# Gating one token quarter early instead of two, and starting the block products one head group later, in a fused attention and gated-MLP kernel

## The chip, the cores and the metric

The kernel runs on one core of one Trainium2 chip. The metric is the device time of one execution in microseconds; less is better. The engines are TensorE (PE, with its weight loads shown apart as PEld), VectorE (DVE), ScalarE (ACT), GpSimd (POOL) and SyncE (SP), whose queue issues nearly all DMAs.

## The reference

2048 tokens of width 512; 32 heads of width 128 over a cache of 2048 keys; all tensors in bf16.

```python
xn = layernorm(x)
# s: attention with cached keys and values
q = (xn @ wq) per head;  p = softmax(q @ k.T * 128 ** -0.5);  s = concat_heads(p @ v) @ wo
# g: silu of a two-stage MLP on the same xn
h  = gelu(layernorm(xn) @ w1), its four column blocks shifted by +1, -1, +2, -2 tokens
x1 = xn + h @ w2
g  = silu(x1 + gelu(layernorm(x1) @ w3) @ w4)
return x + s * g
```

## The kernel before

**Tiling.** Tokens lie in 16 tiles t of 128, and in four quarters qt of 512 (four tiles each). Heads lie in eight groups g of four (HG = 4, NG = 8, QT = 4). One *unit* is one head hh of one group on one quarter: u = 16 g + 4 qt + hh, 128 units, 0 to 127, in that order. A unit has eight *slots* p (SPU = 8), each with two of the 16 key tiles; slot n is 8 u + p.

**Head of the kernel.** The first normalisation, the MLP and its gate g (kept in `xall`, one tile per t, as twice the gate) come first, for quarters 0 and 1 in full; the last matmuls of quarters 2 and 3 (`held_mm`) are spread over the first eight units. When these are done a pool `pS` opens, in which the attention sums live. The queries of units 0 to 10 and 127 are made ahead (`made`).

**A slot of the main loop** (`for n in range(UB * SPU)`, line 904). Two score matmuls into one of two score tiles (`s_slot`), an exp on ScalarE over 1024 columns (L416), and two value matmuls of ten slots earlier (`pv_run`). The rest of a unit's work is placed by slot:

- On VectorE the softmax sums: `add_first` (L422), three `add_next` (L427), `fold` (L431) and `fold_last` (L435), a transpose by DMA, `turned_sums` (L465, L467), a broadcast of the reciprocals by DMA, and `norm` (L485), which scales the value product and frees its bank. For the last four units the sums are taken by four small matmuls on TensorE instead (`sums`, tile ps_sum).
- The queries of a later unit. *Plain:* four matmuls of 512 columns (`q_mm`) and one copy on VectorE (`q_copy`, L327). *Block products:* for a pair of units v, v+1 (two heads), seven products (`product`, k = 1 to 7) of two matmuls with 256 columns each in place of eight, and four steps on VectorE that combine them (`q_part`, six operations, L388 to L400). They need sums of blocks of xn (`x_sum`, L352, four per quarter) and differences of blocks of the weights (`w_sum`, L361, four per pair of heads). Product k = 4 stands one slot after `q_part` 2 (L397, L398), in the odd unit, and writes the bank that this step reads.
- The output projection: once the four heads of a (g, qt) are normalised, one token tile of it is made per unit (`wo_slot`): four matmuls and `wo_post`, which adds the result to `sacc[t]` on VectorE (L537 for the first group, L549 for the others).

Plain queries are placed in slots 3 to 6 two units ahead, up to the pair FIRST. From unit FIRST - 2 to LAST the wo matmuls have places that go round the products; elsewhere they have the default places, slots 3 to 6, and their result is taken in slot 7 or 0.

**The gate in `wo_post`.** With `LATE` and `GY` a quarter can be gated before its last head group. For a tile of a LATE quarter, at group GY - 1 the sum is scaled by the gate (`y_scale`, L515) and the residual added (`y_add`, L520), after its load (`fin_load`), all at later slots, one step of one tile per unit. In the groups from GY on, the wo result is gated on its own (L542) and then added: to the sum (L545) or, in the last group, in `y_out` (L524) when `pay` runs it. For any other tile, the last group does all at once: add (L549), gate (L558), residual (L560), and the output's DMA. Its residual is loaded behind the tile before it (`wo_slot`), the first one when the quarter's last head is normalised (`norm_queue`).

**The end** (from line 971) is an order written out by hand: unit 127 in halves, the last tiles of quarter 2's output projection, and then quarter 3's, whose four tiles have code of their own (`last_stt` to `last_whole`) and always use the early gate.

Every engine runs its instructions in the order in which the program issues them, and so does SP with its DMAs, so an operation that waits holds what was issued behind it.

Of the kernel before, what the change touches and what calls it, by code (L numbers as in the profile page):

```python
# [17 lines left out]
def kernel(  # L18
# [21 lines left out]
    _, H, Sk, Dh = A_k_cache.shape  # L40
# [4 lines left out]
    QT = Sq // 512  # L45
# [5 lines left out]
    HG = 4  # L51
    NG = H // HG

    SPU = KC // 2
# [68 lines left out]
    HEAD = 7  # L123
    XS = 3 * QT + 1
    units = [(g, qt, hh) for g in range(NG) for qt in range(QT) for hh in range(HG)]
    LATE = (QT - 2, QT - 1)
    GY = NG - 2
    NU = len(units)
    TURN = range(NU - HG)
    NS = NU * SPU  # L130
# [3 lines left out]
    def at(n, fn):  # L134
        todo[n].append(fn)
# [201 lines left out]
    def x_block(qt, half, dcs):  # L337
        c = qt * 512 + 256 * half
        return xnT[:, dcs, c:c + 256]

    def x_sum(qt, i):
        if i == 2 and qt < QT - 1:
            out = x_block(qt, 1, LO)
        else:
            out = pS.tile([P, 2, 256], BF16, tag="xs", bufs=XS, name="xs")[:]
        a, b, op = (
            (x_block(qt, 1, LO), x_block(qt, 1, HI), ALU.add),
            (xs.get((qt, 0)), x_block(qt, 0, LO), ALU.subtract),
            (x_block(qt, 0, LO), x_block(qt, 1, LO), ALU.subtract),
            (x_block(qt, 0, HI), xs.get((qt, 1)), ALU.subtract),  # L350
        )[i]
        pin(nc.vector.tensor_tensor(out=out, in0=a, in1=b, op=op))  # L352
        xs[qt, i] = out

    def w_sum(h, i):
        if i == 0:
            wc[h] = pS.tile([P, 4, 2, Dh], BF16, tag="wc", bufs=2, name="wc")
        w, o = wc[h], [wc[h][:, k] for k in range(4)]
        b11, b12, b21, b22 = (wqs[h + j][:, d, :] for d in (LO, HI) for j in (0, 1))
        a, b = ((b12, b11), (b22, o[0]), (b22, b12), (b21, o[1]))[i]  # L360
        pin(nc.vector.tensor_tensor(out=o[i], in0=a, in1=b, op=ALU.subtract))  # L361
# [147 lines left out]
    def fin_load(t):  # L509
        xl = token(False, "xl")  # L510
        pin(nc.sync.dma_start(out=xl[:], in_=xsrc[t]))
        fin[t] = xl
# [20 lines left out]
    def wo_post(g, t, n):  # L533
        ps = wo_box.pop(0)
        if g == 0:
            sacc[t] = pS.tile([P, D], FP32, tag="sacc", bufs=NT, name="sacc")
            pin(nc.vector.tensor_copy(out=sacc[t][:], in_=ps[:]))  # L537
            return
        sa, gl = sacc[t][:], xall[:, t, :]
        if t // 4 in LATE and g >= GY:  # L540
            tm = pS.tile([P, D], FP32, tag="tm", bufs=2, name="tm")
            pin(nc.vector.scalar_tensor_tensor(  # L542
                out=tm[:], in0=ps[:], scalar=0.5, in1=gl, op0=ALU.mult, op1=ALU.mult))
            if g < NG - 1:
                pin(nc.vector.tensor_tensor(out=sa, in0=sa, in1=tm[:], op=ALU.add))  # L545
            else:
                owed.append((t, tm))
            return
        pin(nc.vector.tensor_tensor(out=sa, in0=ps[:], in1=sa, op=ALU.add))  # L549
        if t // 4 in LATE and g == GY - 1:  # L550
            k = n + SPU * (t - 4 * LATE[0]) + 1
            at(max(k - SPU, n + 1), lambda: fin_load(t))
            at(k, lambda: y_scale(t))
            at(k + SPU, lambda: y_add(t))
        if g < NG - 1:
            return
        xl = fin.pop(t)
        pin(nc.vector.scalar_tensor_tensor(  # L558
            out=gl, in0=sa, scalar=0.5, in1=gl, op0=ALU.mult, op1=ALU.mult))
        pin(nc.vector.tensor_tensor(out=xl[:], in0=gl, in1=xl[:], op=ALU.add))  # L560
        pin(nc.sync.dma_start(out=out2d[t * P:(t + 1) * P, :], in_=xl[:]))
# [253 lines left out]
    for g in range(NG - 1):  # L815
        b = (g * QT + QT - 1) * HG
        for hh in range(HG):
            h = (g + 1) * HG + hh
# [35 lines left out]
    def norm_queue(u):  # L854
        norm(u)
        gg, qq, hh = units[u]
        if hh == HG - 1:
            wo_todo.extend((gg, 4 * qq + ts) for ts in range(4))
            if gg == NG - 1 and qq not in LATE:
                fin_load(4 * qq)  # L860
# [3 lines left out]
    def wo_slot(part, n, each=2, **kw):  # L864
# [5 lines left out]
        wo_post(gg, t, n)  # L870
        if gg == NG - 1 and t % 4 < 3 and t + 1 not in fin and t // 4 not in LATE:
            fin_load(t + 1)

    FIRST, LAST = 12, NU - 4
    pairs = range(FIRST, LAST + 1, 2)
    q_plan = defaultdict(list)
    steps = defaultdict(list)
# [9 lines left out]
            if fn is which:  # L887
                fn(v, k)

    for qt, u in ((QT - 1, 8), (0, 10), (1, 14), (2, 18)):  # L890
        for i in range(4):
            at((u + i // 2) * SPU + 1 + 4 * (i % 2), lambda qt=qt, i=i: x_sum(qt, i))
    for h in range(0, H, 2):
        u = (h // HG) * QT * HG + (-4, -2)[h % HG // 2]
        for i in range(4):
            n = max(u, 8) * SPU if h < HG else (u + i // 2) * SPU
            at(n + (2, 6)[i % 2] + (i // 2) * (h < HG) + 8 * (h % HG == 2) * (h < HG), lambda h=h, i=i: w_sum(h, i))

    for v in range(1, NU):
        if v not in made and not FIRST <= v < LAST + 2:  # L900
# [3 lines left out]
    for n in range(UB * SPU):  # L904
        u, p = divmod(n, SPU)
# [65 lines left out]
    n = UB * SPU  # L971
# [156 lines left out]
```

## Time and profile before

| | |
|---|---|
| median of three runs | 1248.7 us (1248.34 to 1249.24) |
| profiled execution | 1248.67 us, of which the instructions span 1246.5 us |
| granted TensorE clock | 1.00 |

Group rows on the page read: line, engine, operation, output and input tiles, shape, count, then busy time and mean duration, then the idle time ahead of them and what ended it. A window row gives busy time and count of instructions for each engine between two moments. In a timeline row stand start, duration, engine, line and what is written and read; brackets hold the idle time before it and its releaser. A row of waits gives the total, the number and the longest.

### The profile page before, as it was taken

Reading aid. Unit: us, or ns where it says so; the run is one execution under the profiler, and the core shown is the slowest. Engines: PE = TensorE matmul, PEld = TensorE weight load, DVE = VectorE, ACT = ScalarE, POOL = GpSimd, SP = SyncE. Lnnn points to the kernel's source line nnn. Section 1 sums busy time; section 2 is a strip of 40 time slices with the busy share of each in tenths; the row PEclk is TensorE's granted clock in tenths of the full one; section 3 lists DMA queues with packets and bytes.
Section 4 is the critical chain, followed back from the end, with each engine's and each line's share of the span. In section 5 each row is a group of like instructions: output and inputs, shape, how many; then the busy total and the mean of one; then the engine's idle time right before and its main releaser. Section 6 shows DMA issues by size and latency. Waiting matters only on the chain.

```text
span 1246.5 us, 17349 instructions
## 1 busy us (share of the span) xinstructions
PE 1224.5 (98%) x6159; PEld 645.3 (52%) x6279; DVE 1091.5 (88%) x1773; ACT 1092.7 (88%) x1127; POOL 26.8 (2%) x75
## 2 busy tenths in 40 slices
PE   9999999999999999999999999999999999999998
PEld 6444444555555555555555555555555555455445
DVE  7712778999999999999999999999999999999997
ACT  6345998999999999999999999999998999899886
POOL 5200000000000000000000000000000000000000
PEclk9999999999999999999999999999999999999999
DMA  7660122443334523443344525563356433443232
GB/s 177 167 149 20 30 39 64 102 95 88 68 73 111 110 44 80 98 103 76 74 85 107 97 48 89 92 113 60 67 99 109 91 75 80 96 102 68 68 74 67
DMA packets 244055, 107.74 MB, mean 86 GB/s; under 512 B 194816, under 2 KB 227712, under 8 KB 243968
## 3 DMA queue, kind: packets, MB, share of 16 engines
q1 hardware_dynamic: 243408, 106.17, 41.7%
q8 instruction: 49, 0.80, 0.3%
q14 instruction: 38, 0.31, 0.1%
q10 hardware_dynamic: 560, 0.46, 0.1%
HBM read 67.50 MB, written 2.36 MB: 56 GB/s over the span
## 4 chain that ended last, share of the span: by engine, by line
PE 73%; DVE 21%; issue 2%; DMA 2%; ACT 1%; SPq 0%; DVEq 0%; ACTq 0%
PE ps_s L112 30%; PE ps_o L112 28%; PE ps_q L112 7%; DVE acc L427 6%; PE ps_wo L112 6%; PE ps_m L112 2%; DVE acc L431 2%; DVE sm L465 2%; DVE oT L485 2%; DVE acc L422 1%; DVE acc L435 1%; DVE sacc L549 1%; DMA rb<-dr 1%; DMA tT<-acc 1%; ACT pT L416 1%
## 5 line engine op out<-in xcount | busy, mean ns | idle before, releaser
L416 ACT ACTIVATE pT<-ps_s 128x1024 bf16<-128x1024 f32 x1016 | 1020.2, 1023 | 81.8 <-PE ps_s L112 45.9
L112 PE MATMUL ps_s<-qT,kT 128*128 128x512 bf16 (+1 forms) x2018 | 599.4, 377 | 0.7
L112 PE MATMUL ps_o<-pT,vb 128*128 128x512 bf16 x1936 | 579.8, 379 | 3.7
L427 DVE TENSOR_TENSOR acc<-acc,pT 128x2048 bf16<-128x2048 bf16 x254 | 306.6, 1207 | 7.1 <-ACT pT L416 6.7
L112 PEld LDWEIGHTS <-kT 128*128 128x128 bf16 x2064 | 232.9, 113 | 144.3 <-issue 1.4
L112 PEld LDWEIGHTS <-vb 128*128 128x128 bf16 x1984 | 193.8, 98 | 216.9 <-issue 0.3
L112 PE MATMUL ps_wo<-wo_h,oT 128*128 128x512 bf16 x484 | 181.9, 379 | 0.5
L422 DVE TENSOR_TENSOR acc<-pT 128x2048 bf16<-128x2048 bf16 x127 | 154.7, 1218 | 17.1 <-ACT pT L416 17.0
L431 DVE TENSOR_TENSOR acc<-acc 128x1024 bf16<-128x1024 bf16 x127 | 87.9, 692 | 4.3
L485 DVE TENSOR_TENSOR oT<-ps_o,rb 128x512 bf16<-128x512 f32 x127 | 86.5, 681 | 1.0 <-DMA rb<-dr 0.7
L465 DVE TENSOR_REDUCE sm<-tT 128x4 f32<-128x512 bf16 x124 | 83.8, 676 | 1.9 <-DMA tT<-acc 1.9
L112 PEld LDWEIGHTS <-oT 128*128 128x128 bf16 x528 | 59.1, 113 | 49.9 <-issue 1.4
L112 PEld LDWEIGHTS <-wc 128*128 128x128 bf16 x456 | 44.5, 98 | 66.7 <-issue 16.0
L549 DVE TENSOR_TENSOR sacc<-ps_wo,sacc 128x512 f32<-128x512 f32 x96 | 65.6, 683 | 0.0
L112 PEld LDWEIGHTS <-wq_h 128*128 128x128 bf16 x394 | 38.5, 98 | 46.4 <-issue 0.9
L400 DVE TENSOR_TENSOR qT<-ps_q,tq 128x512 bf16<-128x512 f32 x57 | 39.4, 691 | 26.3 <-PE ps_q L112 26.0
L435 DVE TENSOR_TENSOR acc<-acc 128x512 bf16<-128x512 bf16 x127 | 54.0, 425 | 4.3
L112 PE MATMUL ps_q<-xnT,wq_h 128*128 128x256 bf16 (+1 forms) x277 | 55.9, 291 | 1.6 <-DVE sacc L537 1.1
L293 ACT ACTIVATE h2T<-ps_s 128x1024 bf16<-128x1024 f32 x28 | 28.7, 1024 | 25.9 <-PE ps_s L112 25.2
L112 PE MATMUL ps_q<-xs,wc 128*128 128x256 bf16 x258 | 49.3, 273 | 0.3
L112 PEld LDWEIGHTS <-w_sb 128*128 128x128 bf16 x368 | 33.5, 98 | 29.6
L112 PE MATMUL ps_s<-xn2T,w_sb 128*128 128x512 bf16 x220 | 48.6, 379 | 0.2
(102 smaller groups left out, 594.9 us busy)
## 6 DMA issues: line engine op xcount, KB each, us to landing
rb<-dr SPq DMA_DIRECT2D x127, 256.0 KB, 4.0
vb<-in_A_v_cache_dram SPq DMA_DIRECT2D x62, 256.0 KB, 3.0
wq_h<-in_A_wq_dram SPq DMA_DIRECT2D x32, 128.0 KB, 3.0
wo_h<-in_A_wo_dram SPq DMA_DIRECT2D x32, 128.0 KB, 2.9
w_sb<-in_B_w_dram SPq DMA_DIRECT2D x8, 256.0 KB, 4.7
kT<-in_A_k_cache_dram SPq DMA_TRANSPOSE x128, 2.9
xl<-in_A_x_dram SPq DMA_DIRECT2D x16, 128.0 KB, 3.1
dr<-rc SPq DMA_DIRECT2D x127, 2.0 KB, 1.4
```

Source lines behind the costliest of these rows:

```text
L112: pin(nc.tensor.matmul(out=out, lhsT=lhsT, rhs=rhs, start=start, stop=stop, **kw))
L293: pin(nc.scalar.activation(out=h2[c, f][:], in_=ps[:], func=ACT.Gelu_apprx_tanh))
L400: pin(nc.vector.tensor_tensor(out=s["q"][:, 1:3, :], in0=ps[:], in1=s["u"][:].unsqueeze(1).to_broadcast([P, 2, 256]), op=ALU.add))
L416: pin(nc.scalar.activation(out=s["pT"][-1][:, jj:jj + 2, :], in_=sps[:], func=ACT.Exp, scale=SCALE))
L422: pin(nc.vector.tensor_tensor(out=s["acc"][:], in0=s["pT"][0][:], in1=s["pT"][1][:], op=ALU.add))
L427: pin(nc.vector.tensor_tensor(out=a[:], in0=a[:], in1=st[u]["pT"][i][:], op=ALU.add))
L431: pin(nc.vector.tensor_tensor(out=a[:, 0:2, :], in0=a[:, 0:2, :], in1=a[:, 2:4, :], op=ALU.add))
L435: pin(nc.vector.tensor_tensor(out=a[:, 0, :], in0=a[:, 0, :], in1=a[:, 1, :], op=ALU.add))
L465: pin(nc.vector.tensor_reduce(out=sm[:], in_=s["tT"][:], axis=mybir.AxisListType.X, op=ALU.add))
L485: pin(nc.vector.tensor_tensor(out=to, in0=o, in1=rb, op=ALU.mult))
L549: pin(nc.vector.tensor_tensor(out=sa, in0=ps[:], in1=sa, op=ALU.add))
```

## The change

Two things change. The LATE quarters are the last one alone instead of the last two, and their sums are gated and given the residual after group 6 instead of group 5 (GY from 6 to 7). The block products begin with unit 16, the second head group, instead of unit 12; units 12 to 15 get plain queries, and the weight sums of the first group go. The block sums, placed before at units 8 and 9 (quarter 3), 10 and 11 (0), 14 and 15 (1), 18 and 19 (2), two to a unit, stand one to a unit from unit 10 to unit 25, in the order of the quarters.

```diff
-    LATE = (QT - 2, QT - 1)
-    GY = NG - 2
+    LATE = (QT - 1,)
+    GY = NG - 1
...
-    FIRST, LAST = 12, NU - 4
+    FIRST, LAST = 16, NU - 4
...
-    for qt, u in ((QT - 1, 8), (0, 10), (1, 14), (2, 18)):
+    for qt in range(QT):
         for i in range(4):
-            at((u + i // 2) * SPU + 1 + 4 * (i % 2), lambda qt=qt, i=i: x_sum(qt, i))
-    for h in range(0, H, 2):
+            at((10 + 4 * qt + i) * SPU + 5, lambda qt=qt, i=i: x_sum(qt, i))
+    for h in range(HG, H, 2):
         u = (h // HG) * QT * HG + (-4, -2)[h % HG // 2]
         for i in range(4):
-            n = max(u, 8) * SPU if h < HG else (u + i // 2) * SPU
-            at(n + (2, 6)[i % 2] + (i // 2) * (h < HG) + 8 * (h % HG == 2) * (h < HG), lambda h=h, i=i: w_sum(h, i))
+            at((u + i // 2) * SPU + (2, 6)[i % 2], lambda h=h, i=i: w_sum(h, i))
```

`wo_post`, which reads `LATE` and `GY`, is unchanged:

```python
        if t // 4 in LATE and g >= GY:
            ...
            if g < NG - 1:
                pin(nc.vector.tensor_tensor(out=sa, in0=sa, in1=tm[:], op=ALU.add))
            else:
                owed.append((t, tm))
            return
        pin(nc.vector.tensor_tensor(out=sa, in0=ps[:], in1=sa, op=ALU.add))
        if t // 4 in LATE and g == GY - 1:
            k = n + SPU * (t - 4 * LATE[0]) + 1
            at(max(k - SPU, n + 1), lambda: fin_load(t))
            at(k, lambda: y_scale(t))
            at(k + SPU, lambda: y_add(t))
```

## The prediction

> **What bounds the kernel now.** I read the page first, then the busy time in windows cut at unit boundaries, then the waits of TensorE, then the timeline of VectorE.
>
> ```profile
> span 1246.5 us, 17349 instructions
> PE 1224.5 (98%) x6159; PEld 645.3 (52%) x6279; DVE 1091.5 (88%) x1773; ACT 1092.7 (88%) x1127; POOL 26.8 (2%) x75
> ```
>
> The profiled execution took 1248.67 us, 2.2 more than its span, and the median of the runs is 1248.7; I work from 1248.67. About 0.2% (2.5 us) is what a measurement of this kernel can tell from no change.
>
> TensorE is the bound on average. VectorE's 88% is spread over a head in which it has little to do and a main part in which it has little left. So I cut the main part into pairs of units, each cut at the first key-tile weight load of an even unit (sixteen such loads make a unit). Columns: start and end, length, then busy time and count for TensorE, its weight loads, VectorE, ScalarE, GpSimd, then the granted clock, DMA share, GB/s.
>
> ```profile
> 201.43:212.19 10.76, 9.61 (x45) 4.68 (x45) 9.06 (x19) 7.97 (x9) 0.00 (x0) 1.00 0.29 61
> 212.19:229.72 17.53, 17.11 (x85) 8.97 (x86) 17.17 (x30) 15.98 (x17) 0.00 (x0) 1.00 0.33 70
> 229.72:246.83 17.11, 17.01 (x86) 9.01 (x87) 16.25 (x28) 16.16 (x17) 0.00 (x0) 1.00 0.50 106
> 246.83:264.79 17.96, 17.33 (x86) 8.99 (x86) 17.60 (x33) 15.99 (x17) 0.00 (x0) 1.00 0.46 94
> 264.79:281.93 17.14, 17.04 (x85) 9.02 (x86) 15.93 (x26) 16.14 (x17) 0.00 (x0) 1.00 0.45 103
> 281.93:299.09 17.16, 17.05 (x85) 9.00 (x86) 16.80 (x29) 15.99 (x17) 0.00 (x0) 1.00 0.49 105
> 333.23:350.30 17.07, 16.96 (x86) 9.03 (x87) 15.73 (x25) 16.15 (x17) 0.00 (x0) 1.00 0.28 68
> ```
>
> These are unit 9, the pairs 10/11, 12/13, 14/15, 16/17, 18/19, and 24/25. The last is the clean pair: 17.07 us, 25 VectorE operations. It holds 86 weight loads, of which 14 belong to half-width block products, so 79 full matmuls' worth: 17.07 / 79 = 0.216 us each, with no stall. Unit 9 and pair 14/15 do TensorE work of the same kind and are longer, with more VectorE operations (33 for 25).
>
> ```profile
> 931.70:1091.07 159.37, 154.50 (x760) 81.03 (x774) 152.22 (x246) 144.55 (x145) 0.00 (x0) 1.00 0.46 90
> 967.30:984.66 17.36, 17.12 (x85) 9.01 (x86) 16.67 (x27) 15.99 (x17) 0.00 (x0) 1.00 0.57 102
> 1091.07:1108.89 17.82, 17.19 (x85) 9.00 (x86) 17.06 (x28) 16.14 (x17) 0.00 (x0) 1.00 0.52 106
> 1108.89:1126.53 17.64, 17.18 (x86) 9.00 (x87) 16.88 (x28) 16.00 (x17) 0.00 (x0) 1.00 0.43 90
> 1126.53:1144.14 17.61, 17.11 (x85) 9.01 (x86) 16.85 (x27) 16.14 (x17) 0.00 (x0) 1.00 0.38 71
> 1144.14:1162.22 18.08, 17.12 (x85) 9.01 (x86) 17.28 (x28) 15.99 (x17) 0.00 (x0) 1.00 0.29 64
> 1162.22:1180.76 18.54, 17.34 (x87) 9.02 (x87) 17.71 (x29) 16.16 (x17) 0.00 (x0) 1.00 0.30 72
> 1180.76:1199.29 18.53, 17.42 (x86) 9.01 (x86) 17.70 (x29) 15.99 (x17) 0.00 (x0) 1.00 0.29 72
> PE ps_q L112 <- DVE qT L398: 7.9, 12, 1.1
> PE ps_q L112 <- DVE sacc L537: 1.1, 1, 1.1
> ```
>
> First the nine pairs 94 to 111 together, then pair 98/99 out of them, then 112/113 to 122/123 one by one. The first wait is the only one of TensorE from 931.70 to 1199.29: a block product stands until VectorE has combined the earlier ones (L398). It falls in the odd unit of a pair, at the product k=4, which comes one slot after the issue of that combination. So VectorE is late, and lateness up to about a slot costs nothing. The second wait is in unit 9: a query matmul waits for a bank that VectorE's copy of a wo result (L537) still holds.
>
> **What an operation costs.** Operations overlap, so the price is start to next start.
>
> ```profile
> 1015.27 0.69 DVE L515 SCALAR_TENSOR_TENSOR sacc<-sacc,xall 128x512 f32<-128x512 f32 x1
> 1015.87 0.42 DVE L397 TENSOR_TENSOR tq<-ps_q,tq 128x256 f32<-128x256 f32 x1
> 1189.85 0.68 DVE L549 TENSOR_TENSOR sacc<-ps_wo,sacc 128x512 f32<-128x512 f32 x1
> 1190.57 0.69 DVE L558 SCALAR_TENSOR_TENSOR xall<-sacc,xall 128x512 bf16<-128x512 f32 x1
> 1191.30 0.42 DVE L560 TENSOR_TENSOR xl<-xall,xl 128x512 bf16<-128x512 bf16 x1
> 1191.64 0.68 DVE L485 TENSOR_TENSOR oT<-ps_o,rb 128x512 bf16<-128x512 f32 x1
> 217.08 0.42 DVE L352 TENSOR_TENSOR xs<-xnT 128x512 bf16<-128x512 bf16 x1
> 217.41 0.42 DVE L388 COPY tq<-ps_q 128x256 f32<-128x256 f32 x1
> ```
>
> A y_scale or y_add costs 0.60. The late finish of a tile that isn't LATE (add, gate, residual) costs 0.72 + 0.73 + 0.34 = 1.79, which is 1.19 over a plain add of 0.60. A block sum (x_sum) costs 0.33.
>
> The room of a pair: in 98/99 two y operations (1.20) made 17.07 into 17.36, so 0.91 was free. In 120/121 two late finishes (2.38) made it 18.54, so 0.91 again. **I take 17.07 + (extra - 0.91).** A pair 16/17 of a group is tighter, by its 26 operations, and a pair 14/15 has w_sums besides and room of about 0.1: pair 14/15 itself has four block sums, three of them (1.0) ahead of the product that waits, and is 0.89 long.
>
> **Units 8 to 25.** Unit 9 loses two block sums and four weight sums, and unit 8 as many ahead of it. That is over 1.8 us of VectorE time ahead of the copy that TensorE waited 1.1 for, so the stall goes; with the pipeline's refill it is 10.76 - 44 x 0.216 = 1.26. **-1.26**.
> Pairs 10/11 and 12/13 become plain: 80 full matmuls instead of 79 with a stall, 17.28 each, so 34.56 for 17.53 + 17.11 = 34.64, -0.08. But the default wo places put queries and wo into slots 3 to 6, and leave four light slots in a row (7, 0, 1, 2) with four matmuls, 0.86 us, each.
>
> ```profile
> 1197.11 17.79 ACT L416 ACTIVATE pT<-ps_s 128x1024 bf16<-128x1024 f32 x17 [1.16 <-PE ps_s L112]
> ```
>
> ScalarE needs 17.79 / 17 = 1.05 per slot, and two score banks cover a little of it. Four light slots lack 4 x 0.18 = 0.7; starting with both banks free I put 0.15 to each of four such runs, +0.60 (bounds: 0, and half of 0.7 each, 1.4). Together **+0.52**. The four query copies that come to VectorE are hidden there: six block operations per pair and the weight sums leave.
> Pair 14/15 keeps one block sum ahead of its waiting product instead of three: 0.33 - 0.1 is left of 0.89, **-0.66**. The sums at 15 and 16 then fall on 16/17: 0.66 against about 0.3 of room, **+0.35**. In 18/19 two sums (0.66) fit, **-0.09**; in 20 to 25 two a pair fit as well, zero (at worst 0.3 in all, if their room is smaller). Sum: **-1.1**, bounds -1.8 and -0.2.
>
> **Units 94 to 123.** Before, sixteen y operations ran one to a unit from 95 to 110, and from 111 to 118 each unit had a LATE chain. After, units 94 to 114 hold nothing beyond the plain add. Nine clean pairs are 9 x 17.07, with 0.07 more for the pair 16/17 of the group: 153.70 for 159.37, **-5.67**. Pair 112/113 goes from 17.82 to 17.14, **-0.68**; 114/115 has one y operation, inside its room, 17.64 to 17.07, **-0.57**; 116/117 has two, 17.61 to 17.36, **-0.25**.
> From 115 to 122 y_scale (odd) and y_add (even) run one to a unit for t 12 to 15. From 119 on they meet the late finishes of the first quarters, which were there before. 118/119: 1.20 + 1.19 = 2.39, so 18.55 for 18.08, **+0.47**. 120/121: 3.58, so 19.74 for 18.54, **+1.20**. 122/123: 2.98, so 19.14 for 18.53, **+0.61**. Sum: **-4.9**. If all of the clean pair's idle 1.34 (17.07 - 15.73) were room, 116 to 123 would be 1.5 shorter, -6.4; if the pile-up in 118 to 123 found 0.5 of room, 1.2 longer, -3.7.
>
> **The end.** The tiles t 8 to 11 are finished here. Before, each had a gate (0.60) and an output add that was put off; now each has 1.79 at once, with a load of the residual (fin_load) and the output's DMA put on SP at once too.
>
> ```profile
> 1220.32 0.68 DVE L542 SCALAR_TENSOR_TENSOR tm<-ps_wo,xall 128x512 f32<-128x512 f32 x1
> 1220.92 0.41 DVE L435 TENSOR_TENSOR acc<-acc 128x512 bf16<-128x512 bf16 x1
> 1222.66 0.27 PE L112 MATMUL ps_sum<-ones_t,acc 128*128 128x1 bf16 x4
> 1225.37 0.69 DVE L542 SCALAR_TENSOR_TENSOR tm<-ps_wo,xall 128x512 f32<-128x512 f32 x1 [0.37 <-PE ps_s L112]
> 1227.96 0.43 DVE L435 TENSOR_TENSOR acc<-acc 128x512 bf16<-128x512 bf16 x1
> 1229.08 0.26 PE L112 MATMUL ps_sum<-ones_t,acc 128*128 128x1 bf16 x4
> 1229.84 0.69 DVE L542 SCALAR_TENSOR_TENSOR tm<-ps_wo,xall 128x512 f32<-128x512 f32 x1 [0.28 <-PE ps_wo L112]
> 1230.45 0.68 DVE L485 TENSOR_TENSOR oT<-ps_o,rb 128x512 bf16<-128x512 f32 x1
> 1236.44 0.17 DVE L596 RECIPROCAL rl<-ps_oh 128x2 f32<-128x2 f32 x1 [2.65 <-PE ps_oh L112]
> xl<-in_A_x_dram SPq DMA_DIRECT2D x16, 128.0 KB, 3.1
> ```
>
> t = 8: the fold (L435) behind it moves from 1220.92 to 1222.11 and ends at 1222.52, just ahead of the column sums at 1222.66: no stall. What follows is 1.19 - 0.60 = 0.59 later, of which the idle 0.37 ahead of t = 9 takes most; 0.2 is left.
> t = 9: the fold ends at 1227.96 + 0.43 + 0.2 + 1.19 = 1229.78, and TensorE wanted to sum at 1229.08. **+0.7**.
> t = 10: the norm behind it (L485) frees the bank in which the last unit's half products start, right after the wo matmuls, at 1231.81 before. It ended at 1231.13; 1.19 later is 0.51 beyond that. **+0.5**.
> t = 11: VectorE stood idle 2.65 before 1236.44, which covers 1.19 and a late load. The loads: SP issues each behind the output of the tile before it, at about 1222.9 for t = 9, so it lands near 1226.0 and is wanted at 1227.0; t = 10 has more, and t = 11 is covered by that idle time. The loads for t 12 to 15 stay on SP ahead of their y operations, later by about twenty units, in windows with a lower DMA share than before; block and weight sums issue no DMA. Sum: **+1.25**, bounds 0.5 (the stalls share one delay) and 2.4 (both chains wholly on the path).
>
> **Sum:** -1.1 - 4.9 + 1.25 = -4.75; 1248.67 - 4.75 = 1243.9 us.
>
> **The rivals.**
> *The pile-up costs more than the rule.* In 118 to 123 VectorE is late at a second place too (the bank that the norm frees for the next unit's value products), and the end costs its upper bound: -1.1 - 3.7 + 2.4 = -2.4, so 1246.3, no change that can be told. For it: the cost rule is fitted on up to 2.38 of extra, and I use it at 3.58. Against: one resource is late, and a stall at the product lets it catch up. 0.18.
> *The residual load becomes the bound, slower.* The load for t is issued only when the tile before is out, and VectorE stands in order at the residual add, with the fold that the sums wait for, or the norm that frees the bank, behind it. It decides from a landing time of about 4.1 us (3.1 plus the 1.0 spare of t = 9). At 7 us for three tiles it costs 3 x 2.9 = 8.7: 1252.6. For it: the queue is in order. Against: the median of 3.1 in the row above, and DMA shares of 0.3 in the last windows. 0.06.
> [...] 0.03.
> [...]
>
> **How the numbers follow.** The forecast has 0.73. Its bounds together are -1.8 - 6.4 + 0.5 = -7.7 (1241.0) and -0.2 - 3.7 + 2.4 = -1.5 (1247.2); the first rival lies inside, the other two (0.09) outside, so the range is 1241.0 to 1247.2. Faster by over 0.2% means below 1246.2: the forecast but for its upper edge (0.69) and a part of the first rival (0.07), 0.76. Within 0.2%: 0.04 and 0.11, 0.15. Slower: 0.09.
>
> **What would show it.** Windows of units 94 to 113 all at 17.07 to 17.14 a pair; unit 9 at 9.5; 120/121 as the longest pair, near 19.7, its wait still on L398; TensorE waiting once at the column sums of unit 126 and once before the half products; the clock 1.00 throughout. It is wrong if pairs 94 to 111 keep more than 17.3 (VectorE's y operations weren't the cause), if the residual add (L560) waits for a DMA in the last 30 us, or if units 10 to 13 take over 36 us together.

## The result, and the profile after

The changed kernel takes 1244.64 us (median of seven, 1243.73 to 1245.28) against 1248.87 for the kernel before beside it: a ratio of 0.9968, 95% interval 0.9956 to 0.9979, so 0.3% faster. The forecast was 1243.9 in 1241.0 to 1247.2. The profiled execution took 1244.64 us too, 4.0 less than that of before.

From the page, and then windows at the same unit boundaries as in the prediction (start and end, length, busy time and count for TensorE, weight loads, VectorE, ScalarE, GpSimd; clock, DMA share, GB/s): unit 9, pairs 10/11, 12/13, 14/15, 16/17, 18/19; units 94 to 111 together; then 112/113 to 122/123.

```profile
span 1242.8 us, 17421 instructions
```
```profile
201.74:211.77 10.03, 9.66 (x46) 4.69 (x45) 7.69 (x12) 7.98 (x9) 0.00 (x0) 1.00 0.36 66
211.77:229.20 17.43, 17.43 (x82) 8.42 (x81) 15.17 (x23) 15.52 (x17) 0.00 (x0) 1.00 0.34 70
229.20:246.63 17.43, 17.43 (x82) 8.44 (x81) 15.61 (x27) 15.52 (x17) 0.00 (x0) 1.00 0.55 99
246.63:264.28 17.65, 17.38 (x87) 9.02 (x86) 17.01 (x30) 15.99 (x17) 0.00 (x0) 1.00 0.53 97
264.28:281.67 17.39, 17.31 (x88) 9.01 (x87) 16.52 (x28) 16.16 (x17) 0.00 (x0) 1.00 0.67 107
281.67:298.73 17.06, 17.06 (x87) 9.01 (x86) 16.23 (x27) 15.99 (x17) 0.00 (x0) 1.00 0.59 102
930.75:1084.57 153.82, 153.82 (x775) 81.11 (x774) 143.38 (x229) 144.63 (x145) 0.00 (x0) 1.00 0.44 86
1084.57:1101.71 17.14, 17.14 (x87) 9.02 (x86) 16.02 (x26) 16.16 (x17) 0.00 (x0) 1.00 0.49 110
1101.71:1119.46 17.75, 17.23 (x88) 8.98 (x86) 16.35 (x27) 16.01 (x17) 0.00 (x0) 1.00 0.74 116
1119.46:1136.83 17.37, 17.23 (x88) 9.02 (x87) 16.68 (x27) 16.16 (x17) 0.00 (x0) 1.00 0.32 65
1136.83:1155.39 18.56, 17.23 (x88) 9.02 (x87) 17.80 (x29) 16.00 (x17) 0.00 (x0) 1.00 0.28 64
1155.39:1175.13 19.74, 17.40 (x88) 9.00 (x86) 18.91 (x31) 16.15 (x17) 0.00 (x0) 1.00 0.40 74
1175.13:1194.27 19.14, 17.53 (x87) 9.00 (x86) 18.31 (x30) 16.00 (x17) 0.00 (x0) 1.00 0.31 70
```

Units 94 to 111 fell by 5.5 us, and TensorE has no idle time in that window. Units 112 to 123 grew from 108.2 to 109.7, all of it from 118 on, where VectorE's count goes up to 31. All waits of TensorE in them are for VectorE, at block products:

```profile
PE ps_q L112 <- DVE qT L398: 4.5, 4, 1.7
PE ps_q L112 <- DVE tq L389: 1.3, 2, 0.7
```

The granted clock is 1.00 in every row, through stalls of up to 1.75 us, the two below both in pair 120/121:

```profile
1162.62 0.38 PE L112 MATMUL ps_q<-xnT,wq_h 128*128 128x256 bf16 x2 [0.59 <-DVE tq L389]
1172.11 0.38 PE L112 MATMUL ps_q<-xnT,wc 128*128 128x256 bf16 x2 [1.75 <-DVE qT L398]
```

| stretch | before | after | change | forecast |
|---|---|---|---|---|
| up to unit 8 | 192.75 | 193.07 | +0.32 | 0 |
| units 8 to 25 | 157.54 | 156.87 | -0.67 | -1.1 |
| units 26 to 93 | 581.40 | 580.81 | -0.59 | 0 |
| units 94 to 123 | 267.59 | 263.53 | -4.06 | -4.9 |
| units 124, 125 | 16.90 | 16.90 | 0 | 0 |
| unit 126 to the end | 30.35 | 31.61 | +1.26 | +1.25 |
| the execution | 1248.67 | 1244.64 | -4.03 | -4.75 |

The stretches add up to the span, -3.7; the last 0.3 lies outside it (the execution is 2.2 us longer than its span before, 1.8 after).

The end, in the timeline of VectorE: tile 9's late finish and the fold behind it, the norm behind tile 10's, tile 11's residual add, and the reciprocal behind it.

```profile
1220.49 0.68 DVE L549 TENSOR_TENSOR sacc<-ps_wo,sacc 128x512 f32<-128x512 f32 x1
1221.21 0.69 DVE L558 SCALAR_TENSOR_TENSOR xall<-sacc,xall 128x512 bf16<-128x512 f32 x1
1221.93 0.43 DVE L560 TENSOR_TENSOR xl<-xall,xl 128x512 bf16<-128x512 bf16 x1
1224.25 0.42 DVE L435 TENSOR_TENSOR acc<-acc 128x512 bf16<-128x512 bf16 x1
1227.32 0.68 DVE L485 TENSOR_TENSOR oT<-ps_o,rb 128x512 bf16<-128x512 f32 x1
1231.55 0.43 DVE L560 TENSOR_TENSOR xl<-xall,xl 128x512 bf16<-128x512 bf16 x1 [2.09 <-DMA xl<-in_A_x_dram]
1232.69 0.17 DVE L596 RECIPROCAL rl<-ps_oh 128x2 f32<-128x2 f32 x1 [0.71 <-PE ps_oh L112]
PE ps_sum L112 <- DVE acc L435: 0.5, 1, 0.5
PE ps_oh L112 <- DVE oT L485: 0.4, 1, 0.4
```

The last two lines are from the waits: TensorE waits once for the fold and once for the norm, 0.9 us in all; before, it had neither wait. The load of tile 11 makes VectorE wait 2.09 us, but it still has to wait 0.71 for TensorE afterwards, so that load is covered, with little to spare.

### The profile page after: what moved, and what is told of

It reads as the page before. It is cut to its first block, busy times and chain, and to the rows that moved or that the text cites. A ratio compares the mean times of both kernels' runs of the same rounds, so it can differ in the third digit from the quotient of the medians.

```text
span 1242.8 us, 17421 instructions
## 1 busy us (share of the span) xinstructions
PE 1230.5 (99%) x6267; PEld 645.0 (52%) x6267; DVE 1081.4 (87%) x1745; ACT 1092.2 (88%) x1127; POOL 26.8 (2%) x75
## 4 chain that ended last, share of the span: by engine, by line
PE 86%; DVE 11%; DMA 2%; ACT 1%; issue 1%; SPq 0%; DVEq 0%; ACTq 0%
PE ps_s L112 35%; PE ps_o L112 33%; PE ps_q L112 7%; PE ps_wo L112 7%; DVE acc L427 3%; PE ps_m L112 2%; DVE oT L485 1%; DVE acc L431 1%; DMA rb<-dr 1%; DVE sm L465 1%; ACT pT L416 1%; DVE sacc L549 1%; DVE xall L558 1%; DVE acc L422 1%; DVE acc L435 1%
## 5 line engine op out<-in xcount | busy, mean ns | idle before, releaser
L112 PE MATMUL ps_s<-qT,kT 128*128 128x512 bf16 (+1 forms) x2064 | 609.1, 377 | 0.0
L112 PE MATMUL ps_o<-pT,vb 128*128 128x512 bf16 x1984 | 589.9, 379 | 0.0
L427 DVE TENSOR_TENSOR acc<-acc,pT 128x2048 bf16<-128x2048 bf16 x254 | 306.9, 1208 | 11.5 <-ACT pT L416 11.2
L112 PE MATMUL ps_wo<-wo_h,oT 128*128 128x512 bf16 x496 | 186.2, 379 | 0.1
L422 DVE TENSOR_TENSOR acc<-pT 128x2048 bf16<-128x2048 bf16 x127 | 154.8, 1219 | 20.4 <-ACT pT L416 20.1
L431 DVE TENSOR_TENSOR acc<-acc 128x1024 bf16<-128x1024 bf16 x127 | 87.9, 692 | 4.3
L549 DVE TENSOR_TENSOR sacc<-ps_wo,sacc 128x512 f32<-128x512 f32 x108 | 73.9, 685 | 0.3 <-PE ps_wo L112 0.3
L112 PE MATMUL ps_q<-xnT,wq_h 128*128 128x256 bf16 (+1 forms) x288 | 61.1, 298 | 1.6 <-DVE tq L389 1.3
```

Source lines behind the costliest of these rows:

```text
L112: pin(nc.tensor.matmul(out=out, lhsT=lhsT, rhs=rhs, start=start, stop=stop, **kw))
L422: pin(nc.vector.tensor_tensor(out=s["acc"][:], in0=s["pT"][0][:], in1=s["pT"][1][:], op=ALU.add))
L427: pin(nc.vector.tensor_tensor(out=a[:], in0=a[:], in1=st[u]["pT"][i][:], op=ALU.add))
L431: pin(nc.vector.tensor_tensor(out=a[:, 0:2, :], in0=a[:, 0:2, :], in1=a[:, 2:4, :], op=ALU.add))
```

## The experiments

Each ratio is to the kernel before, run beside it on the same chip.

**The gate part alone**

```diff
 # the kernel before, with
-    LATE = (QT - 2, QT - 1)
-    GY = NG - 2
+    LATE = (QT - 1,)
+    GY = NG - 1
```

> The kernel before with the gate part alone (LATE the last quarter, GY one group later); block products and sums as before. Theory (a pair of units takes 17.07 us plus what VectorE gets beyond 0.91 us of room, at the place where it gets it): units 94 to 111 as in the changed kernel, 153.8 us for 159.4; units 112 to 123 109.2 to 109.7 for 108.2; the end 1.25 longer; units 8 to 25 unchanged at 157.5. Together 1245.4 to 1245.9 us. Rival (the early block work carries the gain): 1248.0 or more.

1246.21 us, ratio 0.9975 (0.9965 to 0.9985). Units 94 to 111 took 154.1, 112 to 123 109.9, the end 31.62, units 8 to 25 157.7. That is the gate part as it stands in the whole change. The time is 0.3 us above what the theory allowed, and 1.8 below the rival's.

**The blocks part alone**

```diff
 # the changed kernel, with
-    LATE = (QT - 1,)
-    GY = NG - 1
+    LATE = (QT - 2, QT - 1)
+    GY = NG - 2
```

> The kernel before with the blocks part alone (block products from unit 16, block sums one to a unit); the gate as before. Theory: only units 8 to 25 change, by -0.7 us as between the two profiles; 1248.0 us. The gate part and this one add up to the whole change. Rival (the early block work carries the gain): 1245 or less.

1247.61 us, ratio 0.9987 (0.9978 to 0.9996). The parts add up within their intervals: 0.25% and 0.13% for the whole change's 0.32%. In its profile units 8 to 25 took 157.66, no gain on the 157.54 of before: unit 9 was 10.03 as in the whole change, but pair 14/15 took 18.29 instead of 17.65. So this profile does not show where the 0.13% comes from. What goes with such differences comes below.

**Without the last quarter's scaling and residual**

```diff
-            at(k, lambda: y_scale(t))
-            at(k + SPU, lambda: y_add(t))
```

> The changed kernel with the scaling and the residual add (y_scale, y_add) of the last quarter's four tiles left out, so that these tiles come out wrong; the loads stay. It takes 8 VectorE operations from units 115 to 122. Theory: pairs 114/115 and 116/117 go to 17.07, 118/119 to 17.35, 120/121 and 122/123 to 18.5, so units 112 to 123 take 105.7 for 109.7; 1240.6 us. Rival (a VectorE operation is worth the same wherever it goes: 28 fewer brought 4.2 us, so 0.15 each): 1243.4 us.

1241.55 us, ratio 0.9941 (0.9928 to 0.9953). Pairs 116/117 to 122/123:

```profile
1119.22:1136.29 17.07, 17.07 (x88) 8.98 (x87) 15.73 (x25) 16.16 (x17) 0.00 (x0) 1.00 0.30 73
1136.29:1153.96 17.67, 17.23 (x87) 9.03 (x86) 16.75 (x27) 16.00 (x17) 0.00 (x0) 1.00 0.33 67
1153.96:1172.50 18.54, 17.39 (x87) 8.97 (x86) 17.71 (x29) 16.15 (x17) 0.00 (x0) 1.00 0.36 79
1172.50:1191.05 18.55, 17.54 (x88) 9.02 (x87) 17.72 (x29) 16.01 (x17) 0.00 (x0) 1.00 0.27 73
```

Three of the four fall on the rule, 118/119 is 0.3 longer, and the time is nearer the theory's than the rival's. Eight operations out of this stretch were worth 3.35 us here (109.70 to 106.35), 0.42 each, where 28 fewer over the whole kernel brought 4.0. It is the place that counts, not the number.

**The last quarter gated one group earlier**

```diff
-    GY = NG - 1
+    GY = NG - 2
```

> The changed kernel with GY one group earlier, as it was before, but for the last quarter alone. The y operations move from units 115 to 122 to units 99 to 106, where nothing else is extra, and the four wo results of group 6 are gated on their own in units 115 to 118 (0.72 each), 4 operations more in all. Theory: pairs 100 to 105 take 17.36, 0.9 more in all; 114/115 17.07, 116/117 17.6, 118/119 18.1, 120/121 and 122/123 18.5, so units 112 to 123 take 107.0 for 109.7; 1242.8 us. Rival (the count of VectorE operations decides): 4 more, 1245.2 us.

1244.05 us, ratio 0.9962 (0.9949 to 0.9974): four operations more than the changed kernel, and not slower. Its gain on the changed kernel is within the intervals, and the time lies midway between the theory's and the rival's, so it decides nothing; the single pairs do. The pile-up went: 118/119 to 122/123 took 18.08, 18.54 and 18.78 for 18.56, 19.74 and 19.14, and units 112 to 123 107.7. Units 94 to 111 took 156.0, 1.3 over the rule (153.8 and the 0.9 for three pairs). Pairs 100 to 105 are on it (17.37, 17.37, 17.36). Pair 96/97 (17.58) and 108/109 (17.68) are not, and hold these two waits of VectorE for the transposed sums:

```profile
957.58 0.69 DVE L465 TENSOR_REDUCE sm<-tT 128x4 f32<-128x512 bf16 x1 [0.72 <-DMA tT<-acc]
1061.67 0.69 DVE L465 TENSOR_REDUCE sm<-tT 128x4 f32<-128x512 bf16 x1 [0.49 <-DMA tT<-acc]
```

**The finish of tiles 8 to 11 put off**

```diff
 # in wo_post; y_out, run by pay, now gates, adds the residual and sends
-        pin(nc.vector.scalar_tensor_tensor(
-            out=gl, in0=sa, scalar=0.5, in1=gl, op0=ALU.mult, op1=ALU.mult))
-        pin(nc.vector.tensor_tensor(out=xl[:], in0=gl, in1=xl[:], op=ALU.add))
-        pin(nc.sync.dma_start(out=out2d[t * P:(t + 1) * P, :], in_=xl[:]))
+        owed.append((t, xl))
+        if t < 8:
+            pay()
```

> The changed kernel, with the gate, the residual add and the output of tiles 8 to 11 put off to the places where the kernel before ran their output adds; only the add that empties the bank stays at its place. Theory (in the end TensorE waits once for the folded sums and once for the norm, each behind 1.19 us of late finish): both waits go, and the time from unit 126 to the end falls from 31.6 back to 30.4 us; 1243.4 us. Rival (the residual's load or VectorE's total work at the end sets it): it stays at 31.6; 1244.6 us.

Both waits of TensorE went and the end took 30.78 instead of 31.61, 0.4 more than expected. What was left is the load of tile 11, now without cover:

```profile
DVE xl L526 <- DMA xl<-in_A_x_dram: 1.9, 1, 1.9
```

The time was 1245.17 us, ratio 0.9967 (0.9954 to 0.9979): above both forecasts; the 0.8 us that the end shows is less than these runs can tell.

**The last quarter's scaling and residual on GpSimd**

```diff
-        pin(nc.vector.scalar_tensor_tensor(
-            out=sacc[t][:], in0=sacc[t][:], scalar=0.5, in1=xall[:, t, :], op0=ALU.mult, op1=ALU.mult))
+        pin(nc.gpsimd.tensor_scalar(out=sacc[t][:], in0=sacc[t][:], scalar1=0.5, scalar2=None, op0=ALU.mult))
+        pin(nc.gpsimd.tensor_tensor(out=sacc[t][:], in0=sacc[t][:], in1=xall[:, t, :], op=ALU.mult))
...
-        pin(nc.vector.tensor_tensor(out=sacc[t][:], in0=sacc[t][:], in1=xl[:], op=ALU.add))
+        pin(nc.gpsimd.tensor_tensor(out=sacc[t][:], in0=sacc[t][:], in1=xl[:], op=ALU.add))
```

> The changed kernel with the scaling and residual add of the last quarter's tiles on GpSimd (three operations per tile, since the scaling takes two there), at the same slots. Theory: VectorE gets nothing in their place, so units 112 to 123 take 105.7 to 106.4 us as without them; 1241.5 us. Rival (VectorE's operations grow longer while GpSimd works on the same memory): by 0.6 us a tile step or more, so no gain; 1244 us or more.

1245.10 us, ratio 0.9966 (0.9953 to 0.9978); units 112 to 123 took 109.1, where the theory had 105.7 to 106.4. The rival holds. In the timeline of the two engines:

```profile
1122.68 1.86 POOL L516 TENSOR_TENSOR sacc<-sacc,xall 128x512 f32<-128x512 f32 x1
1123.55 1.53 DVE L431 TENSOR_TENSOR acc<-acc 128x1024 bf16<-128x1024 bf16 x1
```

L431 takes 0.69 us in the changed kernel. Here it starts inside GpSimd's operation, takes 0.84 longer and ends 0.54 after that one's end (1122.68 + 1.86 = 1124.54): its last 0.69 us begin at 1124.39, as if it had stood nearly until GpSimd was done. The same comes again 9.2 us later, L516 from 1131.83 for 1.87 and L431 from 1132.72 for 1.53, and L427, begun at 1127.72 inside L520 (1127.01 for 1.48), takes 1.85 where its mean in the changed kernel is 1.21. Not every VectorE operation that overlaps one of GpSimd's is longer: L392 at 1127.38, inside the same L520, takes its usual 0.42, and in the next run, finish_gpsimd, L422 starts inside the scaling (L515) and takes its usual 1.22. L516 and L520 read two tiles and L515 one; whether that decides it no run tested.

```profile
1152.36 1.66 POOL L515 TENSOR_SCALAR sacc<-sacc 128x512 f32<-128x512 f32 x1
1153.38 1.22 DVE L422 TENSOR_TENSOR acc<-pT 128x2048 bf16<-128x2048 bf16 x1
```

**The finish of tiles 0 to 7 on GpSimd as well**

```diff
 # y_gpsimd and finish_later, and in wo_post
+        if t < 8:
+            pin(nc.gpsimd.tensor_scalar(out=sa, in0=sa, scalar1=0.5, scalar2=None, op0=ALU.mult))
+            pin(nc.gpsimd.tensor_tensor(out=gl, in0=sa, in1=gl, op=ALU.mult))
+            pin(nc.gpsimd.tensor_tensor(out=xl[:], in0=gl, in1=xl[:], op=ALU.add))
+            at(n + 6, lambda: pin(nc.sync.dma_start(out=out2d[t * P:(t + 1) * P, :], in_=xl[:])))
```

> The changed kernel with the scaling and residual add of the last quarter's tiles, and the gate and residual add of tiles 0 to 7, on GpSimd, the outputs of these six slots later on SP, and the finish of tiles 8 to 11 put off as in finish_later. Theory: VectorE gets only the plain add in units 112 to 126: 102.7 to 103.5 us for units 112 to 123 instead of 109.7, and 30.4 at the end; 1237 us. Rival (VectorE's operations grow longer while GpSimd works): 1241 us or more.

1246.00 us, ratio 0.9971 (0.9960 to 0.9982); units 112 to 123 took 110.9 and the end 30.6. The rival holds here too. VectorE has 25 operations in pair 120/121 and is as busy as with 31; the two folds are the ones held most (0.69 and 0.43 us in the changed kernel). Window of that pair, then groups over units 112 to 123:

```profile
1156.54:1176.24 19.70, 17.52 (x88) 9.01 (x87) 19.00 (x25) 16.15 (x17) 14.13 (x9) 1.00 0.42 74
L431 DVE TENSOR_TENSOR acc<-acc 128x1024 bf16<-128x1024 bf16 x12 | 13.3, 1112 | 0.4
L435 DVE TENSOR_TENSOR acc<-acc 128x512 bf16<-128x512 bf16 x12 | 9.3, 773 | 0.4
```

**The wo matmuls of units 10 to 13 in other slots**

```diff
+        elif 2 * HG + 2 <= u < FIRST - 2:
+            at_wo = [0, 1, 2, 7]
```

> The changed kernel with the wo matmuls of units 10 to 13 in slots 0, 1, 2 and 7 instead of 3 to 6, where the plain queries stand. Theory (four light slots in a row run at ScalarE's pace): these four units take 8.62 us each instead of 8.72, 34.5 for 34.86; 1244.3 us. Rival (the 0.1 us a unit is something of the plain queries): 34.86 still.

1246.90 us, ratio 0.9979 (0.9970 to 0.9988), an interval that overlaps the changed kernel's. Pairs 10/11 and 12/13 took 17.93 and 18.79, 1.9 us more than in the changed kernel and against both forecasts. The experiment made a wait of its own, since the next tile's first matmul now comes right behind the last tile's result, which VectorE has yet to take from the bank:

```profile
PE ps_wo L112 <- DVE sacc L537: 1.7, 3, 0.7
```

So this run doesn't tell what light slots cost.

**The changed kernel again**

> The changed kernel itself, to have its time beside the next two on the same chip. 0.9968 of the kernel before; the stretches of its first profile (units 94 to 111 in 153.8, 112 to 123 in 109.7, the end in 31.6 us). What differs from that profile by a few tenths in single pairs, if it goes with a wait of VectorE for a DMA (the reciprocals' broadcast rb, the transposed sums tT), is chance and not of the change.

1245.91 us, ratio 0.9970 (0.9959 to 0.9981). The profiled execution was its longest, 1248.11 us. The unit stretches that the change touches late are as in the first profile: 118/119 to 122/123 took 18.56, 19.74, 19.15, and the end 31.72. But units 8 to 25 took 0.8 more, 26 to 93 1.6, 94 to 111 1.0. VectorE's waits for DMAs from unit 8 on, first profile and this one:

```profile
DVE oT L485 <- DMA rb<-dr: 1.5, 3, 0.6
DVE sm L465 <- DMA tT<-acc: 0.7, 2, 0.4
...
DVE sm L465 <- DMA tT<-acc: 3.9, 6, 1.1
DVE oT L485 <- DMA rb<-dr: 2.3, 4, 1.0
```

The same program waits 2.2 us in one execution and 6.2 in another for the transposed sums and the broadcast reciprocals. So single pairs differ by some tenths, and whole executions by two or three us. Up to 1.0 us of the difference may not be this kernel's: the kernel before took 1248.87 beside the first and 1249.91 beside this one.

Where these waits fall is not mere chance. Over all profiles, VectorE waits (over 0.1 us) for the transposed sums in unit 14 in eight of the eleven with the new block work, for the broadcast in unit 17 in eight of them too, and for the broadcast in unit 115 in nine of the eleven with a new gate; in none of the two with the old block work, and none of the two with the old gate, does it wait there. So, as far as two profiles on the other side can show, they came with the change, and their size varies. Why the DMAs land late at these places no run shows.

**Residuals of tiles 8 to 11 loaded early**

```diff
 # finish_later, without the loads of these tiles at their old places, and
+    for i in range(4):
+        at((NU - 5 + i) * SPU + 3, lambda i=i: fin_load(8 + i))
```

> finish_later with the residuals of tiles 8 to 11 loaded one to a unit in units 123 to 126. Theory (with the finish put off, the wait for tile 11's residual was what was left of the longer end, 30.8 for 30.35): the end takes 30.4 us. Rival (the two more operations a tile fill VectorE's idle time at the end): 30.8 still. Time 1.2 us below the changed kernel beside it.

The end took 30.36, as in the kernel before (30.35); no wait for a residual is left. 1245.02 us, ratio 0.9962 (0.9949 to 0.9974), 0.9 below the changed kernel beside it, which the intervals cannot tell from no difference.

**All of these together**

```diff
 # finish_loads, and
-    GY = NG - 1
+    GY = NG - 2
...
-            at((10 + 4 * qt + i) * SPU + 5, lambda qt=qt, i=i: x_sum(qt, i))
+            at((10, 10, 18, 22)[qt] * SPU + i * SPU + (5, 1, 5, 5)[qt], lambda qt=qt, i=i: x_sum(qt, i))
```

> finish_loads with the last quarter gated one group earlier (gate_group6) and the block sums of quarter 1 taken in units 10 to 13 beside those of quarter 0, since the plain units leave VectorE time there and pair 14/15 does not. Theory: pairs 14/15 and 16/17 take 17.07 and 17.14 us; units 112 to 123 about 107.3; units 94 to 111 about 155; the end 30.4. 2.3 us below the changed kernel beside it, if the waits for DMAs do not take some of that back.

1243.32 us, ratio 0.9952 (0.9938 to 0.9965), the fastest of all; the changed kernel beside it took 1245.91, ratio 0.9970. The intervals overlap, so that the two differ is likely and not settled. The end took 30.34, units 112 to 123 107.45 and units 94 to 111 155.3, as expected. Pairs 14/15 and 16/17 took 17.84 and 17.37, over the forecast, with a wait of VectorE for a DMA in each (0.7 and 0.5).

## Why the prediction was right

**What bounds.** VectorE's lateness at the block product behind L398 is what stretches a unit here (4.5 us of TensorE's waits in units 112 to 123); from 120 on, a second product (behind L389, 1.3 us) has a part in it. Taking operations out where they pile up shortened just those pairs (no_y), and moving them shortened them as well (gate_group6).

**The price of a pair**, 17.07 + (extra - 0.91), held beyond the range it was fitted on: 18.55, 19.74 and 19.14 were forecast for 118 to 123, and 18.56, 19.74 and 19.14 measured. The first rival was half right: VectorE is late at a second place in these units, though not at the bank it named, but at the first of the four steps that combine the products (the wait on L389 above). That cost nothing beyond the rule.

**Where the 5.5 us of units 94 to 111 came from.** The prediction took their excess away as a whole. By the price without the weight sums, sixteen y operations would be worth about 2 us there. VectorE's waits for DMAs in 102/103 and 106/107 account for 0.7. The rest is in the pairs that hold weight sums (L361) as well: first pair 94/95 before and after, then 110/111 before, and its operations.

```profile
931.70:949.27 17.57, 17.18 (x86) 9.01 (x87) 16.88 (x30) 15.99 (x17) 0.00 (x0) 1.00 0.52 105
930.75:947.82 17.07, 17.07 (x88) 9.00 (x87) 16.28 (x29) 16.00 (x17) 0.00 (x0) 1.00 0.49 94
1072.77:1091.07 18.30, 17.28 (x86) 8.98 (x86) 17.57 (x31) 15.99 (x17) 0.00 (x0) 1.00 0.36 78
1081.68 0.29 DVE L361 TENSOR_TENSOR wc<-wq_h,wc 128x256 bf16<-128x256 bf16 x1
1081.88 0.69 DVE L542 SCALAR_TENSOR_TENSOR tm<-ps_wo,xall 128x512 f32<-128x512 f32 x1
1082.60 0.69 DVE L545 TENSOR_TENSOR sacc<-sacc,tm 128x512 f32<-128x512 f32 x1
```

A weight sum costs 0.20 from start to start and the LATE chain 0.72 + 0.61 (the next operation starts at 1083.21), 0.73 over a plain add. Pair 94/95 has four weight sums and one y operation, 1.40 of extra, so 17.56 by the price, and 17.07 without the y operation. Pair 110/111 has the chain besides, 2.13, so 18.29. So work that was free by itself had used up the room, and one more operation cost nearly its full length (0.50 of 0.60 in pair 94/95).

**Units 94 to 115.** 153.70 was forecast for units 94 to 111 and 153.82 measured. The term that was mis-sized is pair 114/115, 17.07 forecast and 17.75 measured: VectorE waited for the broadcast there (the one wait of 0.6 us in units 112 to 123) and a y operation had taken room that would have covered more of it. With the wait and no y operation the pair took 17.38 (no_y), with the y operation and no wait 17.09 (gate_alone). The prediction has no such waits anywhere; it lists TensorE's alone.

**Units 8 to 25**, -0.67 for -1.1: unit 9 and pair 14/15 came out 0.5 and 0.3 longer than forecast, units 10 to 13 and pair 16/17 0.3 and 0.1 shorter. The first step that failed is unit 9, said to lose its whole stall: it kept 0.5 of 1.26, by the waits below.

```profile
200.62 1.23 DVE L427 TENSOR_TENSOR acc<-acc,pT 128x2048 bf16<-128x2048 bf16 x1 [0.82 <-ACT pT L416]
206.81 0.38 PE L112 MATMUL ps_q<-xnT,wq_h 128*128 128x512 bf16 x1 [0.37 <-DVE sacc L537]
```

With less to do VectorE stands waiting for ScalarE ahead of that copy, so only part of the 1.8 us taken away arrives. The light slots were put at 0.15 a run and show 0.1 (pairs 10/11 and 12/13 17.43, where 80 matmuls take 17.26 at the 0.2157 from start to start that the others of these two pairs show). In pair 10/11 only four score matmuls start late, by 0.03 and 0.06 in turn, each 0.05 after the end of the exp that frees their tile, as the prediction had it. Pair 14/15 was forecast at 17.31, and what it takes beyond that goes with VectorE's wait for the transposed sums in that pair. Of the profiles with the same operations in it, two have no such wait, and the pair took 17.31 (gate_group6) and 17.29 (y_gpsimd). The changed kernel, its repetition and blocks_alone have these, and took 17.65, 17.95 and 18.29:

```profile
DVE sm L465 <- DMA tT<-acc: 0.3, 1, 0.3
...
DVE sm L465 <- DMA tT<-acc: 0.6, 1, 0.6
...
DVE sm L465 <- DMA tT<-acc: 0.8, 1, 0.8
```

In combined, whose block sum is out of the way there, the wait was 0.7, so its 17.84 does not test the 17.07 expected.

Pair 16/17 looks right by luck: +0.35 was forecast for two block sums beyond the room, and +0.25 measured, but with VectorE's wait of 0.5 for the broadcast. Without that wait the same pair took 17.14 (gate_group6, y_gpsimd, finish_loads), so the sums cost nothing. In the two profiles without either wait, units 8 to 25 took 156.3, 1.3 below before.

**The end**, +1.26 for +1.25: both waits were where the working put them, and with the finish put off and the loads early they were gone (30.36). The agreement to 0.01 is luck: the two terms, 0.7 and 0.5, add up to 1.2, and the waits measured are 0.5 and 0.4.

**What the sum could not hold.** +0.32 ahead of unit 8 and -0.59 in units 26 to 93 are not in the working, and no run ties them to the change. In the other profiles unit 8 starts at 192.8 to 193.3. 0.57 of the latter is pair 78/79, 17.64 before and 17.07 after, where VectorE had waited 0.58 for the transposed sums. That these and the misses in units 8 to 25 and 114/115 come to only 0.7 in all is luck: the profiled execution of the second profile of the changed kernel, 1248.11, lies outside the range of 1241.0 to 1247.2, though the median beside it, 1245.91, lies inside.

The rival of the residual load did not come: one wait of 2.09 us, covered. But that wait, of L560 for a DMA in the last 30 us, was named as a sign of being wrong, and it showed; the sign was too strict, since it left out whether anything waits behind. In finish_later, where the cover was gone, the end was 0.4 longer. Of the chances, 0.03 stand for a fall of the TensorE clock that no run shows: the granted clock was 1.00 in every window above and 0.999 or 1.000 over each execution.

## What to carry to other kernels

Where one engine is full and another nearly so, look for the single instruction at which the second one's lateness stops the first, and count what is queued ahead of it between two such places: work up to the spare time there is free, and all beyond it costs its full length (here 0.91 us a pair was free, and in 120/121 the 3.58 put in cost 2.67). Work that is free today has used up some of that time, so count it too. Once that engine is on time, look for its own waits for DMAs: here they came at places where its lateness had gone. The same number of operations can cost nothing or everything, so spread what can move over the stretches that have room, and put what nobody waits for behind the operation that somebody does. When a difference of a few tenths of a per cent is at stake, profile the same kernel twice before explaining single stretches.

## What was not expected of the hardware

An idle engine was not free help here: in y_gpsimd GpSimd took 1.6 to 1.7 us on average for an operation of the kind that VectorE does in 0.69, and some of VectorE's operations took longer meanwhile (L431 1.53 for 0.69, L427 1.85 for 1.21), so giving it the eight operations (as twelve) brought units 112 to 123 down by 0.6 us, where leaving them out brought 3.35. And VectorE's waits for two kinds of DMA went from 2.2 to 6.2 us between two executions of one program, while its time went from 1244.64 to 1248.11, nearly the whole gain.
